# Attention and feed-forward on one core: 16-bit scores for two more batches, q and k loaded for two heads at a time

## The chip, the cores and the metric

The kernel runs on one core of a Trainium2 chip. The metric is the device time of one execution in microseconds (us). The core has five engines that work through rows of instructions of their own, in order: TensorE (PE, matrix products), VectorE (DVE), ScalarE (ACT), GpSimd (POOL) and SyncE (SP, which here issues the DMA transfers). They wait for one another by semaphores. SBUF is the on-chip memory of 128 partitions; PSUM holds the matrix products in banks.

## The reference

Attention in 8 batches of 8 heads, 576 positions, 64 values a head. A position sees all keys of its own block of 64 and of the blocks ahead of it. The heads' outputs of a position are put side by side (512 values), and a feed-forward layer follows.

```
scores = scale * q @ k^T                 # scale = 1/8
scores = where(block_i >= block_j, scores, -1e9)
attn   = exp(scores - max);  attn = attn / (sum(attn) + 1e-9)
x      = (attn @ v), heads side by side  # 4608 x 512
h      = x @ w_in                        # 512 x 2048
out    = max(0.01*h, h) @ w_out          # 2048 x 512
```

All inputs are 32-bit. q and k are large enough (about 0.57 in spread) that the products are made in several passes or parts.

## The kernel before

**Order.** The kernel is not written in the order in which it runs. `Plan` (lines 97 to 282) is a list scheduler: each piece of work is added with the engines that may do it, a cost in ns on each, a rank and the data it reads and writes. A replay of the costs then chooses engines and the row of instructions of every engine. The ranks are head positions plus constants (`RL` for loads of q and k, `RP` for their preparation, `RB` for late scores, and so on); the costs have constants too (`TURN`, `LOADC`, `TE`). Where the replay finds TensorE idle early in the program it puts in fills: matmuls of `ident` with itself whose result nobody reads (L1337).

**Work.** Batch 0 is done in two sets, "lo" (query rows 0 to 320 of each of the 8 heads) and "hi" (rows 320 to 576), batch 1 as "first" (rows 0 to 192) and "rest" (rows 192 to 576), batches 2 to 7 as "full" heads. The feed-forward layer of finished positions (L1129 and L1165) stands between the heads' work on TensorE. A head's q and k lie with the 64 values of a position on partitions; `z` is the parity of the head and chooses its buffer. Rest and full heads score their last 64 rows in a late block of its own.

**Scores, three ways.** Batch 0 and the first rows of batch 1 are in plain 32 bits, which is four passes a matmul (L696, L702). The host has put q and k on partitions 0 to 63 and again on 64 to 127, and for batch 0 the matmuls of one head go by turns to the two row halves of the array. Rest heads and batch 2 are below `SB` = 3: `before` holds q (`qs`) and k (`kk`) rounded to a 32-bit format with a single pass, high and low part above one another on 128 partitions (copies L328, subtractions L335), and the matmuls run over all 128 rows (L716, L721). Batches 3 to 7 are in 16 bits: two scaled copies and two low parts come from q and k, which the host has stored in both orders, and two DMAs swap the halves of the low part (L644, L645), so that three products of high and low parts run in two row halves at once (L710). Scales for them come from sums of squares of a head: a load of q and k of its own (L1047 squares them), totals over the partitions by two matmuls with `same` and `other` (L1054), once for four heads.

**Masks.** Where the scores are not in 16 bits, a matmul of `upper` with `far` adds a large negative number to the hidden corner (L691). For 16-bit heads VectorE writes the corner with a memset (L738). VectorE then takes row maxima (L747), ScalarE the exponentials (L764), and VectorE splits the normalised result into two 16-bit parts (L811).

**Weights.** Pieces of the two weight matrices come through `raw` and are reduced by ScalarE (L527, L528) and others early in the program; TensorE forms squares of them (L544).

Of the kernel before, what the change touches and what calls it, by code (L numbers as in the profile page):

```python
# [9 lines left out]
F32 = mybir.dt.float32  # L10
F32R = mybir.dt.float32r
# [8 lines left out]
P = 128  # L20
# [10 lines left out]
SIGNS = 3  # L31

# [6 lines left out]
TR = 0.745  # L39
TS = 1.212  # L40
TE = 59.721
# [3 lines left out]
AHEADQ = 5  # L45
RW = -1.068

RL = 4.584
RP = -0.167
RB = 0.488  # L50
RT = 1.469
RV = 2.065
RX = -8.245
RN = -2.665

LEAD = 4.25
LAG = 1.993
RS = 3.005
RG = 0.265
OFF1 = 4.712  # L60
OFF2 = -0.681
SL1 = 12.571
AHEAD = 0.967

LAT = 1550
HOLDP = 456.375
HOLD = 197.235
# [10 lines left out]
TURN = 90  # L78
# [7 lines left out]
SIDE = 34  # L86
STEPA = 0.46
STEPB = 0.457
VD = 3.329
JOINT = 0  # L90
DRATE = 330
SB = 3
RQ = 2.173
RD = 1.608
# [211 lines left out]
def attention_ffn(ctx: ExitStack, tc: tile.TileContext, qk0: bass.AP, qk: bass.AP, v: bass.AP, w_in: bass.AP, w_out: bass.AP, out: bass.AP):  # L306
# [11 lines left out]
    NQ = (B - SB) * H  # L318
# [31 lines left out]
    eighth = fixed([P, 2], F32, "eighth")  # L350
    nc.gpsimd.memset(eighth, 1.0)
    nc.gpsimd.memset(eighth[0:64, 0:1], scale)
    nc.gpsimd.memset(eighth[64:128, 1:2], scale)
# [27 lines left out]
    early = ctx.enter_context(tc.tile_pool(name="early", bufs=1))  # L381
    before = early.tile([P, 6 * S], F32R, name="before", tag="early")
    qs = [before[:, y * S : (y + 1) * S] for y in range(2)]
    kk = [before[:, 2 * (y + 1) * S : 2 * (y + 2) * S].rearrange("p (a b) -> p a b", a=2) for y in range(2)]
# [4 lines left out]
    for y in range(2):  # L389
        nc.gpsimd.memset(kk[y][64:128, 1].bitcast(F32), 0.0)  # L390
        nc.gpsimd.memset(sums[y], 1.0)
        nc.gpsimd.memset(nm[y], 0.0)
# [3 lines left out]
    v_raw = [fixed([P, GROUP, NT * D], F32, "v_raw"), raw.rearrange("p a b -> p (a b)")[:, : GROUP * NT * D].bitcast(F32).rearrange("p (h n) -> p h n", h=GROUP)]  # L396
    junk = fixed([P, GROUP * NT * D], BF16, "junk")
# [23 lines left out]
    for name, n in (("same", P // 2), ("other", P // 2), ("sn", NQ), ("qe", 2 * NQ), ("qsc", 2 * NQ), ("qin", 2 * NQ), ("qx", NQ)):  # L421
        later[name] = ptf[:, at : at + n].bitcast(BF16) if n == P // 2 else ptf[:, at : at + n]
        at += n
    q_raw = [raw.rearrange("p a b -> p (a b)")[:, GROUP * NT * D + S * y : GROUP * NT * D + S * (y + 1)].bitcast(F32) for y in range(3)]
# [41 lines left out]
    after, places, place_keys = [], {}, {}  # L466

    def again(k):
        if not after:
            after.append(early.tile([P, 6 * S], I32, name="after", tag="early"))  # L470
        return after[0][:, k * 2 * CH : (k + 1) * 2 * CH].bitcast(F16)

    found = [(lambda k=k: again(k), [(a, y) for a in ("qs", "kh", "kl") for y in range(2)]) for k in range(6)]
# [106 lines left out]
    def attention(i):  # L580
# [7 lines left out]
        qkt, qkey = qk_in[z], ("qkt", z)  # L588
        plain_s, plain_v = kind in ("lo", "hi", "first"), kind in ("lo", "hi")
        rows = P  # L590
        odd = kind == "lo" and z == 1
        sixteen = kind == "full" and b >= SB
        halves = sixteen or plain_v
        whole = scale if halves else scale / 2
# [17 lines left out]
        qf = qkt.rearrange("p a b -> p (a b)")  # L612
        at = qa if kind == "rest" else 0
        q_in, k_in = qf[:, at : at + nq], qf[:, at + nq : at + nq + ke]

        def load():
            if kind == "first":
                nc.sync.dma_start(qf[:, : 2 * nq].rearrange("p (a b) -> p a b", a=2), qk[b - 1, h][:, :, :nq])
            elif b:
                nc.sync.dma_start(qkt, qk[b - 1, h])  # L620
            else:
# [229 lines left out]
        if not JOINT and kind != "lo":  # L851
            normalise()
# [523 lines left out]
```

## Time and profile before

| | us |
|---|---|
| median of 3 runs | 1017.95 (1016.16 to 1018.43) |
| the profiled execution, its own time | 1018.16 |
| its span | 1016.0 |
| TensorE (PE) busy | 1003.3 (99% of the span) |
| VectorE (DVE) busy | 777.4 (77%) |
| ScalarE (ACT) busy | 729.9 (72%) |
| GpSimd (POOL) busy | 206.9 (20%) |

The span is the time from the first to the last event of the profile; 2.2 us lie around it. Matmuls are pipelined and their ends are modelled, so rows of the time line overlap a little: the time of a block of matmuls is read from its first start to the start of what follows it.

### The profile page before, as it was taken

To read this page: it belongs to the slowest core of one execution; us is meant where nothing else is said; L and a number is where in the kernel's file an instruction comes from. 1 tells how busy PE (TensorE), PEld (TensorE's weight loads), DVE (VectorE), ACT (ScalarE), POOL (GpSimd) and SP (SyncE) were. 2 spreads that over 40 slices of the span, in tenths; PEclk is the share of its full clock that TensorE was granted. 3 is DMA by queue.
4 is the path that set the end of the run, shared out by engine and by line. 5 is a ranking of instruction groups with operands and counts; after the bars stand their busy time and mean duration, and the time that the engine had idled before them with its cause. 6 is when DMAs were issued, how large, how long until landed. Compare 5 with 4: busy or idle time off the path is not lost.

```text
span 1016.0 us, 22617 instructions
## 1 busy us (share of the span) xinstructions
PE 1003.3 (99%) x8538; PEld 711.8 (70%) x8538; DVE 777.4 (77%) x2000; ACT 729.9 (72%) x1718; POOL 206.9 (20%) x279
## 2 busy tenths in 40 slices
PE   8999999999999999999999999999999999999997
PEld 7787766777666666666666666666666666788886
DVE  4688888899998888889988877866667578855454
ACT  4789877788878898888778878776567476533332
POOL 1001221123113334455422201131011021100010
PEclk9999999999999999999999999999999999999999
DMA  7766645988987898787779976883834535100000
GB/s 248 262 224 219 201 125 142 200 194 186 236 190 172 187 216 150 182 206 189 166 165 234 203 163 141 199 168 69 173 80 109 118 66 108 37 12 2 22 21 22
DMA packets 263181, 152.60 MB, mean 150 GB/s; under 512 B 223648, under 2 KB 240032, under 8 KB 263072
## 3 DMA queue, kind: packets, MB, share of 16 engines
q1 hardware_dynamic: 263072, 151.16, 62.9%
q8 instruction: 67, 1.10, 0.5%
q14 instruction: 42, 0.34, 0.1%
HBM read 80.74 MB, written 9.44 MB: 89 GB/s over the span
## 4 chain that ended last, share of the span: by engine, by line
PE 69%; ACT 2%; DVE 0%; issue 0%; DVEq 0%; ACTq 0%
PE p_h L1129 30%; PE p_o L1165 23%; PE p_s L710 5%; PE p_t L941 3%; PE p_o L1257 3%; PE p_s L1257 2%; PE p_t L963 2%; ACT slab L764 0%; ACT junk L1047 0%; ACT prow L764 0%; ACT slab L328 0%; PE p_s L721 0%; DVE slab L1270 0%; DVE ob L1270 0%; ACT junk L1019 0%
## 5 line engine op out<-in xcount | busy, mean ns | idle before, releaser
L1165 PE MATMUL p_o<-woh,ring 128*128 128x512 f16 x960 | 281.1, 379 | 0.0
L1129 PEld LDWEIGHTS <-wih 128*128 128x128 f16 x2432 | 226.3, 98 | 68.1 <-issue 17.1
L1165 PEld LDWEIGHTS <-ring 128*128 128x128 f16 (+1 forms) x1440 | 134.9, 98 | 135.4 <-issue 11.8
L1129 PE MATMUL p_h<-slab,wih 128*128 128x256 f16 (+1 forms) x1152 | 185.8, 267 | 0.0
L1129 PE MATMUL p_h<-xh,wih 128*128 128x256 f16 (+1 forms) x640 | 168.4, 268 | 1.4 <-ACT g L1134 1.3
L1134 ACT ACTIVATE g<-p_h 128x512 f32<-128x512 f32 (+1 forms) x152 | 86.8, 572 | 115.0 <-PE p_h L1129 112.1
L1129 PE MATMUL p_h<-xh,wil 128*128 128x256 f16 (+1 forms) x640 | 168.1, 267 | 0.0
L1129 PE MATMUL p_h<-xl,wih 128*128 128x256 f16 (+1 forms) x640 | 168.1, 267 | 0.0
L1129 PE MATMUL p_h<-slab,wil 128*128 128x256 f16 (+1 forms) x576 | 150.7, 267 | 0.0
L747 DVE TENSOR_REDUCE nm<-p_s 128x1 f32<-128x192 f32 (+4 forms) x308 | 137.4, 484 | 14.3 <-PE p_s L691 12.0
L1165 PE MATMUL p_o<-wol,ring 128*128 128x512 f16 x480 | 142.7, 379 | 0.0
L1129 PEld LDWEIGHTS <-wil 128*128 128x128 f16 x1216 | 118.9, 98 | 12.3
L336 POOL TENSOR_TENSOR ring<-g,ring 128x512 bf16<-128x512 f32 (+1 forms) x46 | 55.1, 1197 | 177.6 <-ACT ring L325 97.7
L811 DVE SCALAR_TENSOR_TENSOR slab<-prow,rec,slab 64x64 f16<-64x64 f32 (+4 forms) x148 | 80.7, 565 | 5.8 <-ACT slab L807 5.4
L335 DVE TENSOR_TENSOR ring<-g,ring 128x512 bf16<-128x512 f32 (+1 forms) x82 | 54.8, 668 | 33.0 <-ACT ring L325 32.4
L811 DVE SCALAR_TENSOR_TENSOR slab<-slab,rec 128x448 f16<-128x448 f32 (+4 forms) x132 | 73.3, 578 | 3.5 <-ACT slab L807 3.1
L764 ACT ACTIVATE slab<-p_s,nm,ptf 128x448 f32<-128x448 f32 (+4 forms) x100 | 60.5, 610 | 3.2 <-DVE nm L756 2.0
L764 ACT ACTIVATE prow<-p_s,nm,ptf 128x448 f32<-128x448 f32 (+4 forms) x100 | 60.4, 609 | 3.1 <-DVE nm L756 2.1
L325 ACT CAST ring<-g 128x512 f16<-128x512 f32 (+1 forms) x101 | 59.6, 591 | 1.9
L941 PEld LDWEIGHTS <-vs 128*128 128x128 f16 x968 | 49.6, 98 | 9.2 <-issue 4.6
L710 PE MATMUL p_s<-slab 64*128 64x320 f16 (+2 forms) x720 | 54.8, 276 | 0.0
L941 PE MATMUL p_t<-slab,vs 128*128 128x128 f16 (+1 forms) x968 | 54.2, 209 | 0.1
(234 smaller groups left out, 1725.1 us busy)
## 6 DMA issues: line engine op xcount, KB each, us to landing
qk_in<-in_qk SPq DMA_DIRECT2D x56, 576.0 KB, 4.6
raw<-in_qk SPq DMA_DIRECT2D x40, 288.0 KB, 3.5
raw<-in_w_in SPq DMA_DIRECT2D x16, 512.0 KB, 4.3
raw<-in_w_out SPq DMA_DIRECT2D x16, 512.0 KB, 4.4
slab<-slab SPq DMA_DIRECT2D x80, 72.0 KB, 4.3
out<-ob SPq DMA_DIRECT2D x19, 256.0 KB, 2.3
v_raw<-in_v SPq DMA_DIRECT2D x7, 640.0 KB, 4.5
raw<-in_v SPq DMA_DIRECT2D x7, 640.0 KB, 4.5
```

The lines of the kernel that those rows point to most:

```text
L325: one = lambda: nc.scalar.copy(dst(), src())
L335: ("DVE+" if sb else "DVE", dve(n) + 65, lambda: nc.vector.tensor_sub(dst(), one(), two())),
L336: ("POOL", pool2(n) - (0.25 * n if n == 512 else 0), lambda: nc.gpsimd.tensor_sub(dst(), one(), two())),
L710: go = lambda ap=ap, cols=cols, k0=k0, k1=k1, q_of=q_of, k_of=k_of, half_=half_, first=first, last=last: nc.tensor.matmul(ap, q_of[half_, ...
L747: [("DVE", dve(kw[t]), lambda t=t, ap=ap, flat=flat: nc.vector.tensor_reduce(nm[z][: qn[t], t : t + 1], ap[: qn[t]], axis=AX.X if flat els ...
L764: nc.scalar.activation(o, ap[: qn[t]], AF.Exp, bias=nm[z][: qn[t], t : t + 1], scale=whole if plain_s else esc[: qn[t]] if sixteen else 1. ...
L811: ("DVE+", dve(w) + 62, lambda: nc.vector.scalar_tensor_tensor(part(1), p, by, part(0), op0=ALU.mult, op1=ALU.subtract)),
L941: nc.tensor.matmul(p_t[x][:, c : c + src.free_size()], vs[z][:, (j + 1) % NT], src, start=start, stop=stop)
L1129: nc.tensor.matmul(hh[:, i, :n], w[:, f, d, :], x[:, d, :n], start=k == 0, stop=k == len(terms) - 1)
L1134: add([("ACT", act(2 * n), lambda: nc.scalar.activation(g[z][:, :, :n], hh[:, :, :n], AF.Prelu, alpha=0.01, scale=DOWN))], rank, [("h", z) ...
L1165: nc.tensor.matmul(p_o[m], a[:, i, m * P : (m + 1) * P], w[:, 2 * u + i, :], start=u == 0 and k == 0, stop=u == NU - 1 and k == 5,)
L1257: nc.tensor.matmul(acc(n), a[:, s, :], x()[w], start=u == 0 and k == 0, stop=u == NU - 1 and k == len(terms) - 1)
```

## The change

q and k come in a new layout from the host. For batch 0 and for the first 192 rows of batch 1 (`in_qk0`, `in_qk1`) each head lies on 64 partitions, and the kernel loads it to partitions 0 to 63 or 64 to 127 by its parity (`lanes`), into `spare`; the score matmuls use that half (`g = z`). For batches 1 to 7 q lies over k on 128 partitions, and one load brings two heads (`pair_in`, which takes the place of `q_group`) to one of three buffers. The same load serves the squares and the scores. The copies in the other order, the 32-bit tile `before` with its successor `after`, and the "side" layout of the scores are gone; a tile `spare` takes their place.

For every rest and full head one scaled copy `top` and one low part `low_` are made, and two DMAs of 64 partitions each swap the halves of both parts at once (576 positions of two 16-bit parts, 144 KB a transfer where 72 KB was before). Batches 1 and 2 score in 16 bits as the others do, with memsets as masks. Totals are formed for two heads at a time. New values of the rank and cost constants set another order of all instructions.

```
-TE = 59.721
+TE = 67.487
-RL = 4.584
+RL = 5.274
-HOLD = 197.235
+HOLD = 33.841
-TURN = 90
+BACK = 60
+TURN = 110
-SB = 3
...
-    early = ctx.enter_context(tc.tile_pool(name="early", bufs=1))
-    before = early.tile([P, 6 * S], F32R, name="before", tag="early")
+    spare = fixed([P, 6 * 2 * CH], I32, "spare")
+    qk_0 = [spare[:, 832 * y : 832 * (y + 1)].bitcast(F32) for y in range(2)]
...
-        sixteen = kind == "full" and b >= SB
-        halves = sixteen or plain_v
+        sixteen = not plain_s
...
+        qf, lanes = qk_0[z], slice(64 * z, 64 * z + 64)
...
+            nc.sync.dma_start(qf[lanes, : nq + ke], qk1[h] if kind == "first" else qk0[h, :, o : o + nq + ke])
...
-            add(copying(S, lambda: sx2, lambda: qkt[:, 1], by=cross), rp, [qkey, ("qsc", eq)], [k2])
-            add(copying(S, lambda: sx1, lambda: qkt[:, 0], by=mine), rp, [qkey, ("qsc", eq)], [k1])
...
-            add([("SP", 475, lambda: nc.sync.dma_start(sx3[0:64], sx4[64:128]))], rp, [k4], [k3], lag=dma(S * 64 * 2))
-            add([("SP", 475, lambda: nc.sync.dma_start(sx3[64:128], sx4[0:64]))], rp, [k4], [k5], lag=dma(S * 64 * 2))
...
-            add(copying(qe - qa, lambda: qd, lambda: q_in, by=eighth[:, 0:1]), rp, [qkey], [("qs", z)])
-            add(copying(ke, lambda: khd, lambda: k_in, by=eighth[:, 1:2]), rp, [qkey], [("kh", z)])
-            add(subtracting(qe - qa, lambda: qd[64:128], lambda: q_in[64:128], lambda: qd[64:128]), rp, [qkey], [("qs", z)])
-            add(subtracting(ke, lambda: kld[0:64], lambda: k_in[0:64], lambda: khd[0:64]), rp, [qkey, ("kh", z)], [("kl", z)])
+            add(copying(S, lambda: top, lambda: mine, by=by), rp, [qkey, ("qsc", eq)], [k1])
+            add([("DVE+", dve(S) + 62, lambda by=by: nc.vector.scalar_tensor_tensor(
+                low_, mine, by, top, op0=ALU.mult, op1=ALU.subtract
+            ))], rp, [qkey, ("qsc", eq), k1], [k2])
+            for y in range(2):
+                at, to = 64 * y, 64 - 64 * y
+                add([("SP", 475, lambda at=at, to=to: nc.sync.dma_start(qk16[z][to : to + 64, 2:4], qk16[z][at : at + 64, 0:2]))], rp, [k1, k2], [moved[y]], lag=dma(S * 64 * 4))
+            upside, low_side = (top, turned_[0]), (low_, turned_[1])
...
+                g = b if sixteen else z
...
-        for k in range(GROUP):
-            y = (GROUP * e + k) % 3
...
+        add([("SP", 475, lambda: nc.sync.dma_start(buf, qk[b - 1, h // 2]))], rank, [], [key] + first, lag=1.2 * dma(2 * S * P * 4))
+        add([("ACT", act(2 * S, True) + 94, lambda: nc.scalar.activation(
+            junk[:, : 2 * S], buf.rearrange("p a b -> p (a b)"), AF.Square, accum_out=sn[:, one]
+        ))], rank + RD, [key, "blocks"], [("sn", e), "junk"])
```

In the order of the program TensorE's fills go from 61 to 51 matmuls, the pairs of totals from 10 to 28, the squares of q and k from 40 operations on 576 columns to 28 on 1152, the loads for them from 40 to none beside the 28 of two heads, and the swaps from 80 to 112. In the new file the same statements have lower line numbers: L664 are all score matmuls and mask matmuls, L703 the exponentials (L764 before), L686 the maxima (L747), L750 the splitting (L811), L1047 the feed-forward's first product (L1129), L509 and L510 the weight pieces on ScalarE (L527, L528), L614 the low part, L679 the mask memsets, L1255 the fills (L1337).

The first excerpt is TensorE's row at the first scores of a rest head of batch 1; `slab_80` is the tile of the 16-bit parts. Before:

```order
L1129 MATMUL p_h_144<-slab_85,wil 128x256
L721 MATMUL p_s<-before 128x448 x2
L721 MATMUL p_s<-before 128x320 x2
L691 LDWEIGHTS upper
L691 MATMUL p_s<-far__78,upper 128x64
L691 LDWEIGHTS upper
L691 MATMUL p_s<-far__78,upper 128x64
L1129 LDWEIGHTS wih
```

After, at the same place:

```order
L1047 MATMUL p_h_135<-slab_81,wil 128x256
L664 LDWEIGHTS slab_80
L664 MATMUL p_s<-slab_80 128x320
L664 LDWEIGHTS slab_80
L664 MATMUL p_s<-slab_80 128x448
L664 LDWEIGHTS slab_80
L664 MATMUL p_s<-slab_80 128x320
L664 LDWEIGHTS slab_80
L664 MATMUL p_s<-slab_80 128x448
L664 LDWEIGHTS slab_80
L664 MATMUL p_s<-slab_80 128x320
L664 LDWEIGHTS slab_80
```

Four 128-row matmuls and two mask matmuls have become six matmuls in alternating row halves (the sixth stands behind the excerpt), with nothing else between.

The second excerpt is VectorE's row between two heads of batch 1; `p_s` is the score bank, `qk_in` the loaded q and k. Before:

```order
L335 TENSOR_TENSOR ring<-g_148,ring 128x512
L747 TENSOR_REDUCE nm_107<-p_s 128x1
L811 SCALAR_TENSOR_TENSOR slab_84<-prow_89,rec_111,slab_84 128x448
L335 TENSOR_TENSOR before<-qk_in_99,before 64x576 x2
L783 RECIPROCAL rec_111<-rec_111 128x1
```

After (the reduction of `nm_101` is the late one of a head, and the low part behind it belongs to the head after the next, which has the same buffer):

```order
L679 MEMSET p_s 64x64
L330 TENSOR_TENSOR ring<-g_139,ring 128x512
L686 TENSOR_REDUCE nm_101<-p_s 128x1
L614 SCALAR_TENSOR_TENSOR slab_81<-qk_in_95,ptf,slab_81 128x576
L750 SCALAR_TENSOR_TENSOR slab_81<-slab_81,rec_105 128x448
L750 SCALAR_TENSOR_TENSOR slab_81<-slab_81,rec_105 128x320
L722 RECIPROCAL rec_105<-rec_105 128x1
L679 MEMSET p_s 64x2x64
```

The low part has taken the place of the two subtractions, and memsets of the masks stand ahead of the reductions.

The third excerpt is the start of ScalarE's row; `prow` holds the first head's exponentials, `slab` and `raw` there are the first weight pieces. Before:

```order
L764 ACT_TABLE_LOAD
L764 ACTIVATE prow_88,sums_109<-p_s,nm_107 128x320
L764 ACTIVATE prow_87,sums_109<-p_s,nm_107 128x192
L764 ACTIVATE prow_86,sums_109<-p_s,nm_107 64x64
L527 ACTIVATE slab_84<-raw 128x512
```

After:

```order
L509 ACT_TABLE_LOAD
L509 ACTIVATE slab_80<-raw 128x512
L510 ACTIVATE raw<-raw 128x512
L703 ACTIVATE prow_84,sums_102<-p_s,nm_100 128x320
L703 ACTIVATE prow_83,sums_102<-p_s,nm_100 128x192
```

The first weight piece and the table load have moved ahead of the first exponentials.

## Rows read from the trace of the kernel before

**Rows 1.** Busy time by windows: us, PE, PEld, DVE, ACT, POOL, clock, DMA, GB/s.

```profile
20.00:140.00 120.00, 118.69 (x962) 93.13 (x962) 97.33 (x252) 100.56 (x248) 15.19 (x16) 1.00 0.64 204
140.00:300.00 160.00, 157.48 (x1286) 112.36 (x1284) 145.90 (x346) 129.12 (x309) 32.46 (x36) 1.00 0.86 191
```

**Rows 2.** Waits of TensorE, the longest entry: us in total, times, longest.

```profile
PE p_s L721 <- ACT slab L764: 2.2, 2, 1.3
```

**Rows 3.** TensorE's time line at a rest head: start, us, operation, count.

```profile
178.82 0.93 PE L721 MATMUL p_s<-before 128*128 128x448 f32 x4
179.60 0.23 PE L691 MATMUL p_s<-far__78,upper 128*128 128x64 bf16 x2
179.67 0.59 PE L1165 MATMUL p_o<-woh,ring 128*128 128x512 f16 x2
...
183.43 0.78 PE L721 MATMUL p_s<-before 128*128 128x288 f32 x4
...
184.09 0.59 PE L1165 MATMUL p_o<-woh,ring 128*128 128x512 f16 x2
```

**Rows 4.** The same at heads of batch 2, late block first.

```profile
247.08 0.38 PE L721 MATMUL p_s<-before 128*128 128x288 f32 x1
...
247.84 0.38 PE L1165 MATMUL p_o<-woh,ring 128*128 128x512 f16 x1
...
251.55 1.27 PE L721 MATMUL p_s<-before 128*128 128x448 f32 x6
...
252.77 0.27 PE L1129 MATMUL p_h<-xh,wih 128*128 128x256 f16 x1
```

**Rows 5.** The same at 16-bit heads of batch 3, late block first.

```profile
316.04 0.54 PE L710 MATMUL p_s<-slab 64*128 64x288 f16 x6
316.51 0.39 PE L1165 MATMUL p_o<-woh,ring 128*128 128x512 f16 x1
...
333.89 0.83 PE L710 MATMUL p_s<-slab 64*128 64x320 f16 x12
334.65 0.18 PE L1021 MATMUL p_t<-vn,ones 128*128 128x1 bf16 x1
```

**Rows 6.** The same in batch 0, a lo and a hi head.

```profile
28.80 0.80 PE L696 MATMUL p_s<-qk_in 64*128 64x320 f32 x6
...
29.57 0.33 PE L872 MATMUL p_t<-ident,prow 128*128 128x128 f32 x1
...
58.01 1.13 PE L696 MATMUL p_s<-qk_in 64*128 64x224 f32 x8
...
59.13 0.43 PE L918 MATMUL p_t<-ptf,vf 128*64 128x256 f32 x1
```

**Rows 7.** The same, attention times v of a hi head.

```profile
91.85 1.90 PE L918 MATMUL p_t<-ptf,vf 128*64 128x256 f32 x10
```

**Rows 8.** The same, a stretch of fills, and a pair of totals.

```profile
23.88 1.50 PE L1337 MATMUL p_o<-ident 128*128 128x128 f32 x12
...
309.38 0.20 PE L1054 MATMUL p_t<-ptf 128*128 128x4 bf16 x2
309.44 0.38 PE L1165 MATMUL p_o<-woh,ring 128*128 128x512 f16 x1
```

**Rows 9.** ScalarE's time line, its first instruction.

```profile
6.71 1.28 ACT L764 ACT_TABLE_LOAD   x1 [6.71 <-PE p_h L691]
```

**Rows 10.** Instructions of lines 721 and 641: ns min/median/max, first and last start.

```profile
L721 PE MATMUL p_s<-before x148: 191/309/554, 147.8 to 304.5; 128*128 128x288 f32 x64, 128*128 128x448 f32 x32, 128*128 128x320 f32 x32, 128*128 128x192 f32 x16
...
L641 DVE SCALAR_TENSOR_TENSOR slab<-qk_in,ptf,slab x40: 757/816/1381, 292.8 to 836.9; 128x576 f16<-128x576 f32 x40
```

**Rows 11.** DMA issues (KB, median us to landing), and line 645's landings.

```profile
qk_in<-in_qk SPq DMA_DIRECT2D x56, 576.0 KB, 4.6
...
slab<-slab SPq DMA_DIRECT2D x80, 72.0 KB, 4.3
...
DMA to landing us min/median/max: 2.0/4.2/7.0
```

More of the change, by code (lines that the diff above doesn't have):

```diff
@@ L724, in scores @@
-                yield RATE * (k1 - k0), go, LOADS
-        def softmax(tiles, mms, masks, r, sides=None):
+                    q_of, k_of = upper[half_], far[half_]
+                elif plain_s:
+                    q_of, k_of = q_in[half_, cols], k_in[half_, k0:k1]
+                else:
+                    cols = slice(q0[t], q0[t] + P)
+                    q_of, k_of = (low_side if c == 1 else upside)[b][half_, cols], (low_side if c == 2 else upside)[1 - b][half_, k0:k1]
+                go = lambda ap=ap, q_of=q_of, k_of=k_of, first=first, last=last: nc.tensor.matmul(ap, q_of, k_of, start=first, stop=last)
@@ L727, in softmax @@
+                yield price, go, TURN if y == 0 else LOADS if plain_s and t is not None else LOADC
+        def softmax(tiles, mms, masks, r):
             banks = sorted({(sk, bk) for _, _, bk in tiles for bk in bk})
@@ L828, in attention @@
         alias = ([6, 7] if z else [5, 4]) if kind == "first" else range(NT)
-        side = kind == "full" and i >= SIDE and not sixteen
-        order = "side" if side else f"first{z}" if kind == "first" else kind
+        order = f"first{z}" if kind == "first" else kind
         lay = order_a.get(order, ())
@@ L1025, in v_group, with pair_in @@
         add([("DVE+", 68, second)], rank, [("ve", e)], [("vin", e)])
-    def q_group(e):
-        i0 = next(i for i, (n, kind) in enumerate(work) if n == SB * H + GROUP * e and kind == "full")
+    def pair_in(e):
+        i0 = next(i for i, (n, kind) in enumerate(work) if n == H + 2 * e and kind in ("rest", "full"))
         b, h = divmod(work[i0][0], H)
         rank = pos[i0] - RL - RQ
-        same, other, sn, qe, qsc, qin, qx = later.values()
+        same, other, sn, qe, qsc, qx = later.values()
         if e == 0:
@@ L1051, in q_group @@
         x = bank()
         def total(y):
-            nc.tensor.matmul(p_t[x][:, GROUP * y : GROUP * y + GROUP], (same, other)[y], tops(sn[:, cols]), start=True, stop=True)
-        add([("PE", [(30, lambda y=y: total(y), LOADH) for y in range(2)])], rank + RD, [("sn", e, k) for k in range(GROUP)] + ["blocks"], [("t", x)])
-        add([("DVE", 75, lambda: halved(qe[:, two].bitcast(I32), p_t[x][:, : 2 * GROUP]))], rank + RD, [("t", x)], [("qe", e)])
-        first, second = powers(lambda: qe[:, two].bitcast(I32), lambda: qsc[:, two], lambda: qin[:, two])
@@ L1059, in q_group @@
-        add([("DVE+", 75, first)], rank + RD, [("qe", e)], [("qsc", e)])
-        add([("DVE+", 75, second)], rank + RD, [("qe", e)], [("qin", e)])
-        a, z = slice(two.start, two.start + GROUP), slice(two.start + GROUP, two.stop)
+            nc.tensor.matmul(p_t[x][:, y : y + 1], (same, other)[y], tops(sn[:, one]), start=True, stop=True)
+        add([("PE", [(30, lambda y=y: total(y), LOADH) for y in range(2)])], rank + RD, [("sn", e), "blocks"], [("t", x)])
+        add([("DVE", 75, lambda: halved(qe[:, two].bitcast(I32), p_t[x][:, :2]))], rank + RD, [("t", x)], [("qe", e)])
@@ L1358 @@
         "in_qk0": qk0,
+        "in_qk1": qk1,
         "in_qk": qk,
```

233 lines of the change are left out of this document (74 added, 159 removed).

## The prediction

> **What bounds the kernel now.** I read the busy time by stretches of the span first, then the list of TensorE's waits, then single score blocks on the time line of TensorE. TensorE is the bound nearly everywhere: it is busy 118.69 of the 120 us from 20 to 140 us and 157.48 of the 160 us from 140 to 300 us [rows 1]. VectorE, with 145.90 of 160 us, is the only other engine that comes close, and only in that second stretch. The longest entry in the list of TensorE's waits is 2.2 us, in two waits of the scores of batches 1 and 2 for an exponential that still holds the score bank [rows 2]. So a cost counts where it lands on TensorE's own row of instructions; work taken off ScalarE, VectorE or the DMA queues is worth only such waits as these. Everything below is therefore a sum over TensorE's row: the time from the first matmul of a block to the first one behind it, before and after.
>
> **Part a: scores of batch 1 (the eight "rest" heads) and batch 2 go to 16 bits.** Before, they are single-pass matmuls of rounded 32-bit data on all 128 rows. The block of a rest head takes 0.85 us (178.82 to 179.67) and its late block, the last 64 rows, 0.66 us (183.43 to 184.09) [rows 3]. A head of batch 2 takes 1.22 us (251.55 to 252.77) and 0.76 us (247.08 to 247.84) [rows 4]. Eight of each: 8 x (0.85 + 0.66) + 8 x (1.22 + 0.76) = 27.9 us. After, all sixteen run as the heads of batches 3 to 7 run already, three products, each in alternating 64-row halves: 0.76 us for the block of four row tiles (333.89 to 334.65) and 0.47 us for the late one (316.04 to 316.51) [rows 5]. Those blocks have 1536 and 864 columns per half, so a column costs (0.76 - 0.47) / 672 = 0.43 ns, and a rest head, with 1344 columns per half, comes to about 0.68 us. No mask matmuls remain; VectorE writes the masks. After: 8 x (0.76 + 0.47) + 8 x (0.68 + 0.47) = 19.0 us. **Part a: -8.9 us.** These heads' rows are known on both sides, so I put no more than 1 us of doubt on it.
>
> **Part b: batch 0 loses the second row half.** This part is easy to miss, since the diff speaks of a load. Batch 0 scores in plain 32 bits, four passes a matmul. Before, q and k lie on both halves of the partitions, and the score banks of one head are worked on in both row halves by turns: 0.77 us for 576 columns (28.80 to 29.57) and 1.12 us for 1024 columns (58.01 to 59.13) [rows 6]. After, a head's q and k lie on one half only (the half is the parity of the head), and all its score matmuls follow one another there. The trace has no 32-bit score block in one half. Its nearest row is another 32-bit four-pass block in one stretch of the array, the attention-times-v matmuls of batch 0: 1024 columns in a row that is 1.90 us long [rows 7]. Such a row is 0.07 us longer than the time to the next block's start, as rows 5 show (0.83 against 0.76), so 1.83 us, 1.79 ns a column. With 0.07 us for the two mask matmuls (179.60 to 179.67, rows 3), a "lo" head comes to 576 x 1.79 ns + 0.07 = 1.10 us and a "hi" head to 1.90 us. Bounds: below, no change, if the halves were no help before; above, twice the old block, if they were a full help, 8 x (0.77 + 1.12) = +15.1 us. I take the nearest row: 8 x (1.10 + 1.90) - 15.1 = **+8.9 us**, which is what part a brings.
>
> **Part c: totals.** A head's largest possible value is bounded from sums of squares. Two small matmuls form the totals: 0.06 us (309.38 to 309.44) [rows 8]. They come once for two heads now (28 times) and came once for four (10 times): 18 x 0.06 = **+1.1 us**.
>
> **Part d: fills.** The plan puts matmuls with no use into TensorE's row where it believes the engine idle. There are 61 of them in the order before and 51 after, and one in the order is two in the trace. Twelve take 1.50 us (23.88) [rows 8], so twenty are worth 2.5 us if useful work takes their place and nothing if a wait does. From 20 to 140 us TensorE lost only 1.3 us of 120 [rows 1], so what stood there was mostly due already; I take **-2.0 us**, between 0 and -2.5.
>
> **Part e: the start.** ScalarE loads its table for 1.28 us at 6.71 us, right when the first scores are done, and TensorE's transposes wait for the exponential behind it [rows 9]. In the new order the table load belongs to the first weight piece, ahead of the first scores. That can hide all of it (-1.3), or, if that piece lands late, put it and the piece's two operations (about the length of that load once more) ahead of the first exponential (+2). The loads for the first head are half as large. I take **-1.0 us**.
>
> **Part f: waits in batches 1 and 2.** The two waits of 2.2 us [rows 2] are of scores for a bank. The new scores stand in the same place, with fewer copies on ScalarE ahead of the exponentials; I take half, **-1.1 us**, between 0 and -2.2. What is next late there is VectorE, which loses two subtractions a head and gains one operation of 0.82 us [rows 10] and short mask writes. Fewer and larger loads, and 28 squares instead of 40 on ScalarE, I cost at nothing: they lie behind TensorE's row, which has work of the feed-forward layer while they run; if that cover went, each would cost a wait of its own length, 4.6 us for a load [rows 11].
>
> **The sum.** -8.9 + 8.9 + 1.1 - 2.0 - 1.0 - 1.1 = -3.0 us against the profiled execution's 1018.16 us: 1015.2 us. That execution is 0.2 us above the median of the runs shown, so the forecast is 1015.0 us. About 0.2%, 2 us, is what a measurement of this kernel can tell from no change: faster is below 1015.9, slower above 1020.0.
>
> **Rival 1, slower: the swaps are late.** In batches 1 and 2 the scores could start right behind the last copy; now they wait for two DMAs that swap halves of both 16-bit parts, issued behind the low part. The scores of those sixteen heads run from 147.8 to 304.5 us [rows 10], 9.8 us a head. In the order after, the low part of a head stands right behind the late reduction of the head that used the same buffer, so there is about one such period for 0.82 us of VectorE and the swap's flight: 9.0 us are left for the flight. Swaps of half the size land after 4.3 us in the middle and 7.0 us at most [rows 11]: a new one waits only if its flight grows with its size. Then the middle one takes 8.6 us and the longest 14.0, and the wait decides from 9.0 us on. With half of the sixteen heads late by 1 us in the mean that is +8 us, 1023.0 us. Against it: a load of eight times the bytes lands in 4.6 us [rows 11], so a flight does not go by bytes alone. For it: the DMA share is highest in this stretch, 0.86 [rows 1]. Behind TensorE's waiting score matmuls stand the feed-forward matmuls, so the wait costs its full length.
>
> The Trainium skill, "DMA: Bandwidth & Descriptors", section "Rules for kernel authors", speaks against two transfers to disjoint partition halves: it says that they share the same engines and so serialize, and advises one 128-partition transfer. By it the second swap would land a transfer behind the first. The trace shows nothing of it at half the size: the second swap lands after 4.2 us in the middle, both kinds together after 4.3 [rows 11].
>
> **Rival 2, more gain: neighbouring heads overlap.** Neighbours of batch 0 now lie in opposite row halves, so where two heads' score blocks stand next to each other the array could run them at once, as it ran the two halves of one head before. In the order after, two pairs of lo heads stand so. A pair then takes 2 x 0.77 instead of 2 x 1.10 us [rows 6, 7]: 2 x 0.66 = 1.3 us less, 1013.7 us. Against it: the pair's second head comes as a block behind the whole first one, not by turns, and the starts in the trace keep the order of the program, so little of it is side by side. The Trainium skill, "TensorEngine Tiling (Array Packing)", section "Tiling Modes", says that different tiles can load weights and multiply in parallel; by that rule the pairs would overlap. The trace bears it out only within a head, 0.77 us for 576 columns [rows 6].
>
> **Rival 3, no gain: the start is later.** The first weight piece lands behind the first scores, and the table load with its two operations stands ahead of the first exponential: +2.0 in place of -1.0, 1018.0 us. TensorE has nothing else to do then but fills and weight squares.
>
> **Rival 4, slower: part b costs its upper bound.** If one row half takes twice the old block, +15.1 in place of +8.9 us: 1021.2 us. Against it: the 1.79 ns a column of rows 7.
>
> **How the numbers follow.** The forecast has 0.50 (0.31 of it faster, 0.18 within, 0.01 slower), rival 1 0.20 (slower), rival 2 0.10 (faster), rival 3 0.15 (0.13 within, 0.02 slower), rival 4 0.05 (slower). That is faster 0.41, same 0.31, slower 0.28. The likeliest case's own range is 1011 to 1019: the sum with fills and waits at their better ends and part b 2 us lower, or with fills, waits and start at their worse ends. The range of 8 in 10 takes rival 1 in and goes down to parts a, b, d and f at their better ends together with rival 2: 1009 to 1024.
>
> **What would show it.** Right: a block of batch 0 takes 1.10 and 1.90 us in TensorE's time line, one of batches 1 and 2 0.76 or 0.68 and 0.47; no TensorE wait on a swap; table load before 5 us. Wrong: waits of the score line on the swap's DMA or on the low part between 140 and 300 us (rival 1); new waits anywhere behind 300 us, which I have at nothing; a lo block far from 1.10 us, the least certain price of the sum.

## The result, and the profile after

| | us | |
|---|---|---|
| median before | 1018.19 | 1016.16 to 1019.51, 4 runs |
| median after | 1032.56 | 1030.73 to 1033.03, 4 runs |
| ratio | 1.0139 | 95% interval 1.0126 to 1.0151 |

The changed kernel is 14 us slower; 3 us less were forecast, and 1024 was the upper end of the range. The profiled execution took 1032.97 us, with a span of 1031.0. Its first page says that TensorE is still the bound; the last matmul ends at 1025.40 us, and at 1010.35 in the kernel before.

The busy time by windows of the changed kernel (us, PE, PEld, DVE, ACT, POOL, clock, DMA, GB/s), as in rows 1, with the stretch behind them:

```profile
20.00:140.00 120.00, 120.00 (x884) 93.85 (x883) 96.51 (x239) 95.44 (x234) 12.42 (x13) 1.00 0.58 173
140.00:300.00 160.00, 157.71 (x1324) 100.57 (x1323) 132.41 (x366) 127.08 (x292) 46.37 (x56) 1.00 0.72 148
300.00:860.00 560.00, 555.30 (x4770) 361.10 (x4768) 450.09 (x1191) 418.04 (x1006) 162.66 (x204) 1.00 0.67 136
```

TensorE gets through 884 matmuls from 20 to 140 us, 962 in the kernel before [rows 1], and is busy all the time. VectorE is relieved from 140 to 300 us (132.41 against 145.90), the DMA share falls from 0.86 to 0.72, and nothing of that shows in the time. From 300 to 860 us TensorE idles 4.7 us, and 0.12 us in the kernel before:

```profile
300.00:860.00 560.00, 559.88 (x4777) 364.16 (x4776) 440.06 (x1177) 432.31 (x1032) 144.83 (x186) 1.00 0.72 158
```

TensorE's waits after, in all more than 0.5 us (us in total, times, longest), as in rows 2:

```profile
PE p_h L1047 <- DVE slab L1030: 2.8, 3, 1.6
PE p_s L664 <- ACT slab L703: 2.0, 6, 0.7
PE p_t L800 <- ACT prow L703: 1.4, 1, 1.4
PE p_o L1255 <- POOL ident masks.py:199: 1.4, 1, 1.4
PE p_t L974 <- DVE slab L832: 1.0, 1, 1.0
...
PE p_s L664 <- ACT prow L703: 0.7, 3, 0.3
PE p_t L869 <- DMA slab<-slab: 0.6, 2, 0.4
```

The longest single wait stands in the feed-forward rows, for VectorE's split of x, and the granted clock falls right behind it. TensorE's time line at that place, and the clock by windows:

```profile
353.45 0.37 PE L1047 MATMUL p_h<-slab,wih 128*128 128x256 f16 x1 [1.58 <-DVE slab L1030]
```

```profile
353.50:356.90 3.40, 3.40 (x25) 2.68 (x25) 3.27 (x7) 2.28 (x7) 2.37 (x3) 0.50 0.41 104
```

For these 3.4 us TensorE is at the lower of its two levels (1.2 of 2.4 GHz), and its matmuls take 1.6 us more than the same kinds do elsewhere in the trace (an estimate from their median distances). In the profile of the kernel before, the clock stays at its upper level from 12.7 to 1012.8 us.

No score matmul (L664) waits for a swap. The DMA issues (KB, median us to landing), as in rows 11:

```profile
slab<-slab SPq DMA_DIRECT2D x112, 144.0 KB, 3.8
qk_in<-in_qk SPq DMA_DIRECT2D x19, 576.0 KB, 5.2
raw<-in_qk SPq DMA_DIRECT2D x9, 576.0 KB, 5.0
```

A swap of twice the size lands after 3.8 us, sooner than the old one's 4.3 [rows 11].

The time line of TensorE at a lo and a hi head of batch 0, as in rows 6:

```profile
39.10 1.30 PE L664 MATMUL p_s<-spare 64*128 64x320 f32 x6
...
40.38 0.32 PE L853 MATMUL p_t<-ident,rec 64*64 64x64 f32 x2
...
47.68 1.99 PE L664 MATMUL p_s<-spare 64*128 64x224 f32 x8
...
49.66 0.33 PE L800 MATMUL p_t<-ident,prow 128*128 128x128 f32 x1
```

The lo block takes 1.28 us (0.77 before) and the hi block 1.98 us (1.12 before). Two lo heads side by side, in opposite row halves, take 2.25 us; the other such pair stands at the very start and waits for its load:

```profile
23.57 1.19 PE L664 MATMUL p_s<-spare 64*128 64x320 f32 x5
...
25.82 0.38 PE L1255 MATMUL p_o<-ident 128*128 128x128 f32 x1
```

And how a block of scores is entered, a late block of the last rest head (a late block has the last 128 query rows of a head, 448 to 576, not 64) and a main block of batch 2 in the changed kernel:

```profile
235.94 0.27 PE L1047 MATMUL p_h<-xh,wil 128*128 128x256 f16 x1
236.14 0.54 PE L664 MATMUL p_s<-slab 64*128 64x288 f16 x6
236.62 0.39 PE L1083 MATMUL p_o<-woh,ring 128*128 128x512 f16 x1
...
240.42 0.27 PE L1047 MATMUL p_h<-xh,wil 128*128 128x256 f16 x1
240.62 0.83 PE L664 MATMUL p_s<-slab 64*128 64x320 f16 x12
241.38 0.29 PE L869 MATMUL p_t<-slab,vs 128*128 128x128 f16 x2
```

and in the kernel before, the matmul ahead of the block of rows 3:

```profile
178.79 0.27 PE L1129 MATMUL p_h<-slab,wil 128*128 128x256 f16 x1
```

The blocks themselves are as forecast, 0.48 and 0.76 us; the main block of a rest head takes 0.67 us (157.98 to 158.65). But the first half-row matmul starts 0.20 us behind the start of the last 256-column feed-forward matmul, where the next feed-forward matmul would start 0.11 us behind it. The old full-row block starts 0.03 us behind it (178.79 to 178.82). A time from a block's first start to the next block's start leaves this out on one side and counts a piece of the feed-forward matmul in on the other. The distance goes with the part of the array that comes next: in both traces every undisturbed matmul of 128 rows and 128 columns but the single-pass 32-bit ones starts 0.11 us behind a 256-column feed-forward matmul, whatever its line and type, and the ones on a part of the array start 0.20 us behind it, the score matmuls in half rows as well as the transposes in half columns (L925, then L853).

Added up over TensorE's whole row (from each matmul's start to the next one's, by kind; the sum is the 15.05 us by which the last matmul ends later):

| kind | before | after | |
|---|---|---|---|
| score and mask matmuls | 98.7 | 101.4 | +2.7 |
| of it batch 0 | 16.3 | 27.6 | +11.3 |
| of it rest heads and batch 2 | 28.4 | 19.5 | -8.8 |
| feed-forward matmuls (L1129, L1165; then L1047, L1083) | 697.4 | 708.8 | +11.4 |
| fills | 20.2 | 18.1 | -2.0 |
| last matmuls of attention times v (L963; then L891) | 27.5 | 29.5 | +2.0 |
| totals | 0.6 | 1.7 | +1.1 |
| the rest | 164.4 | 164.3 | -0.1 |

The feed-forward matmuls are the same 5088. Their +11.4 us are, by the distance of each start to the next: +6.2 us at the change to scores, waits there counted in (before, 74 entries into half rows, each 0.096 us more than a plain distance, +7.1 us, and 31 into full rows, most of them 0.08 or 0.19 us less but three with a wait, +0.2 us together; after, 104 into half rows, +13.5 us, and none into full rows), +4.6 us inside the feed-forward rows (3.6 us of waits and 1.0 us of the slower clock from 353.5 us), and 0.6 us at other changes. The +2.0 us behind attention times v are waits of what comes next, 1.5 us of them two waits of a pair of totals (L974), whose result needs a bank that VectorE has not yet emptied (L832).

### The profile page after: what moved, and what is told of

It reads as the page before. It is cut to its first block, busy times and chain, and to the rows that moved or that the text cites. A ratio compares the mean times of both kernels' runs of the same rounds, so it can differ in the third digit from the quotient of the medians.

```text
span 1031.0 us, 22658 instructions
## 1 busy us (share of the span) xinstructions
PE 1014.0 (98%) x8584; PEld 705.9 (68%) x8584; DVE 785.3 (76%) x2054; ACT 717.8 (70%) x1683; POOL 238.5 (23%) x308
## 5 line engine op out<-in xcount | busy, mean ns | idle before, releaser
L1083 PE MATMUL p_o<-woh,ring 128*128 128x512 f16 x960 | 279.4, 380 | 0.1
L1047 PEld LDWEIGHTS <-wih 128*128 128x128 f16 x2432 | 225.5, 98 | 66.1 <-issue 18.8
L1083 PEld LDWEIGHTS <-ring 128*128 128x128 f16 (+1 forms) x1440 | 133.4, 98 | 141.3 <-issue 15.2
L1047 PE MATMUL p_h<-slab,wih 128*128 128x256 f16 (+1 forms) x1152 | 187.1, 268 | 2.8 <-DVE slab L1030 2.8
L1047 PE MATMUL p_h<-xh,wih 128*128 128x256 f16 (+1 forms) x640 | 168.7, 268 | 0.0
L1047 PE MATMUL p_h<-xh,wil 128*128 128x256 f16 (+1 forms) x640 | 168.3, 267 | 0.0
L1047 PE MATMUL p_h<-xl,wih 128*128 128x256 f16 (+1 forms) x640 | 168.3, 267 | 0.0
L1047 PE MATMUL p_h<-slab,wil 128*128 128x256 f16 (+1 forms) x576 | 151.4, 268 | 0.0
L686 DVE TENSOR_REDUCE nm<-p_s 128x1 f32<-128x192 f32 (+4 forms) x308 | 137.0, 484 | 16.3 <-PE p_s L664 13.5
L1083 PE MATMUL p_o<-wol,ring 128*128 128x512 f16 x480 | 142.8, 379 | 0.0
L1047 PEld LDWEIGHTS <-wil 128*128 128x128 f16 x1216 | 119.0, 98 | 15.9 <-issue 3.3
L331 POOL TENSOR_TENSOR ring<-g,ring 128x512 bf16<-128x512 f32 (+1 forms) x55 | 69.0, 1254 | 112.9 <-ACT ring L320 67.5
L703 ACT ACTIVATE slab<-p_s,nm,ptf 128x448 f32<-128x448 f32 (+4 forms) x132 | 81.2, 620 | 18.5 <-DVE nm L695 17.2
L703 ACT ACTIVATE prow<-p_s,nm,ptf 128x448 f32<-128x448 f32 (+4 forms) x132 | 81.2, 619 | 12.4 <-DVE nm L695 9.9
L750 DVE SCALAR_TENSOR_TENSOR slab<-prow,rec,slab 128x192 f16<-128x192 f32 (+4 forms) x148 | 83.5, 588 | 4.6 <-ACT slab L746 4.3
L664 PE MATMUL p_s<-slab 64*128 64x320 f16 (+2 forms) x960 | 76.1, 279 | 2.9 <-ACT slab L703 2.0
L750 DVE SCALAR_TENSOR_TENSOR slab<-slab,rec 64x64 f16<-64x64 f32 (+4 forms) x132 | 74.4, 587 | 4.2 <-ACT slab L746 3.9
L664 PEld LDWEIGHTS <-slab 64*128 64x128 f16 x960 | 38.4, 94 | 43.3 <-issue 30.8
L320 ACT CAST ring<-g 128x512 f16<-128x512 f32 (+1 forms) x109 | 64.5, 592 | 2.3
L330 DVE TENSOR_TENSOR ring<-g,ring 128x512 bf16<-128x512 f32 (+1 forms) x73 | 47.0, 644 | 17.8 <-ACT ring L320 17.1
```

What stands on the lines that cost most here:

```text
L320: one = lambda: nc.scalar.copy(dst(), src())
L330: ("DVE+" if sb else "DVE", dve(n) + 65, lambda: nc.vector.tensor_sub(dst(), one(), two())),
L331: ("POOL", pool2(n) - (0.25 * n if n == 512 else 0), lambda: nc.gpsimd.tensor_sub(dst(), one(), two())),
L664: go = lambda ap=ap, q_of=q_of, k_of=k_of, first=first, last=last: nc.tensor.matmul(ap, q_of, k_of, start=first, stop=last)
L686: [("DVE", dve(kw[t]), lambda t=t, ap=ap, flat=flat: nc.vector.tensor_reduce(nm[z][: qn[t], t : t + 1], ap[: qn[t]], axis=AX.X if flat els ...
L703: nc.scalar.activation(o, ap[: qn[t]], AF.Exp, bias=nm[z][: qn[t], t : t + 1], scale=scale if plain_s else esc[: qn[t]] if sixteen else 1. ...
```

## The experiments

The theory after the result was A: the loss is the price of matmul blocks, batch 0's single row half (10 to 11 us) and the entries into half rows, which take back most of the gain of the 16-bit scores, with some waits on top. The rival B: the blocks matter little and the new order of instructions loses the time.

**Batch 2 in 16 bits, alone, in the kernel before.**

```
-SB = 3
+SB = 2
```

> The kernel before with one number changed, SB = 2: batch 2 (8 heads) scores in 16 bits in two row halves, with the old loads and swaps; the rest heads of batch 1 stay as they were. Theory A (getting into a block of half-row matmuls costs what getting into a full-row block does not): in the traces of before and after, the first half-row score matmul starts 205 ns behind the start of the last 256-column feed-forward matmul, 312 ns behind a 512-column one, while the single-pass full-row one of before starts 28 ns behind it, so that a block read from its first start flatters the half-row kind by about 0.23 us. Then 8 x ((1.16 + 0.77) - (0.76 + 0.47)) = 5.6 us less, but 16 x 0.23 = 3.7 us of it goes into the entries: about 2 us faster, 1016. Rival B (the blocks' own times are right and the loss of the changed kernel is elsewhere): 5.6 us faster, 1012.6.

Measured: 1017.62 against 1018.53 us, ratio 0.9997 (0.9981 to 1.0012), so no change. In TensorE's row the score blocks are 5.3 us shorter, as their own times say, the feed-forward matmuls 4.7 us longer, of which 2.2 stand at the entries, waits there counted in (74 to 87 into half rows, 31 to 13 into full rows), and 2.5 are waits elsewhere in these rows. The gain that I read from the rows of blocks is there and is given back at the change of mode and in waits. Theory A had 2 us of gain, which is outside the interval by a little; new waits at other places (1.5 us for a transfer of P, 0.8 us for totals of v) are of the size of the rest.

**What the change between half and full rows costs.** A matmul of zeros stands in the middle of each 16-bit score block, once over all rows, once over the block's own half.

```
...
                 yield price, go, ...
+                if sixteen and y == 2:
+                    yield RATEH * BLK, lambda ap=ap, rows=slice(0, P): nc.tensor.matmul(ap[:, 0:BLK], zero[rows], far[rows], start=False, stop=False), LOADC
```

> The changed kernel with one more matmul of zeros, 128 rows by 64 columns, behind the third matmul of every 16-bit score block (112 blocks); it adds nothing to the scores, but the array goes from half rows to full rows and back. Theory A (a change between half and full rows has a price of 0.1 to 0.2 us): 112 x 0.15 to 0.3 = 17 to 34 us more, 1050 to 1066. Rival B (no such price): 112 x 0.03 = 3 us, 1036.

> The control of the run with the full-row zeros: the same matmul at the same place, but on the 64 rows of the block's own half, so the array stays in half rows. Both theories: 112 x 0.03 = 3 us more, or less where it hides beside the other half: 1032 to 1037.

Measured: 1065.54 us with the full-row zeros (ratio 1.0464, 1.0441 to 1.0487) and 1035.82 with the half-row ones (1.0172, 1.0152 to 1.0193). Over the changed kernel that is 33 us, 0.29 us for each of 112, against 3.3 us, 0.03 us each. The time line of a block with full-row zeros:

```profile
248.21 0.39 PE L666 MATMUL p_s<-slab 64*128 64x320 f16 x3
248.53 0.20 PE L669 MATMUL p_s<-far__76,zero 128*128 128x64 bf16 x1
248.66 0.64 PE L666 MATMUL p_s<-slab 64*128 64x64 f16 x9
249.23 0.60 PE L1087 MATMUL p_o<-woh,ring 128*128 128x512 f16 x2
```

and with half-row zeros:

```profile
243.66 0.39 PE L666 MATMUL p_s<-slab 64*128 64x320 f16 x4
243.89 0.19 PE L669 MATMUL p_s<-far__76,zero 64*128 64x64 bf16 x1
243.90 0.62 PE L666 MATMUL p_s<-slab 64*128 64x448 f16 x8
244.45 0.60 PE L1087 MATMUL p_o<-woh,ring 128*128 128x512 f16 x2
```

The same block takes 1.02 against 0.79 us, so going to full rows and back costs 0.23 us more than the same 64 columns in the block's own half. Over the whole kernel the difference of the two runs is 29.7 us, 0.27 us a block; some 2 us of it is the granted clock, which stands at its lower level for 10.2 us with the full-row zeros and 6.8 us with the half-row ones. A full-row matmul of 64 columns is not what costs; going there and back is. The Trainium skill has a rule for this: "TensorEngine Tiling (Array Packing)", section "Tiling Modes", says that a change of tiling mode drains the engine. The trace agrees and gives the price here, 0.1 us to enter half rows and 0.23 us there and back.

**Batch 0's row halves.** First with a new plan for it (a head's matmuls by turns in both halves, and the plan counting so):

```
-                g = b if sixteen else z
+                g = b if sixteen or plain_v else z
...
```

> The changed kernel with batch 0 again on both row halves: its q and k are loaded to all 128 partitions, and a head's score matmuls go by turns to both halves. All else as changed. Theory A: the block of a lo head goes back from 1.29 to 0.77 us and of a hi head from 1.98 to 1.13, 8 x (0.52 + 0.85) = 11 us less: 1021.6. Rival B (the new order of instructions is what loses; a shorter block only lengthens waits behind it): less than half of that, above 1027.

Measured: 1041.74 us, ratio 1.0225 (1.0205 to 1.0245), 9 us more than the changed kernel. The blocks did get shorter (a lo head 0.76, a hi head 1.13 us), but the planned order had 164 fill matmuls in the trace in place of 102, and the waits grew:

```profile
PE p_h L1047 <- DVE slab L1030: 6.0, 2, 3.2
PE p_s L664 <- ACT slab L703: 5.8, 6, 3.6
PE p_t L974 <- ACT junk L968: 1.5, 1, 1.5
```

It also lost by the clock. By windows:

```profile
261.90:268.70 6.80, 5.41 (x42) 3.71 (x41) 5.25 (x13) 2.50 (x6) 0.00 (x0) 0.50 0.73 183
354.10:371.10 17.00, 9.61 (x65) 5.47 (x65) 13.00 (x43) 14.62 (x35) 9.40 (x14) 0.50 0.45 106
```

The first stretch begins inside a wait of 2.8 us, the second inside one of 3.6 us. The matmuls in them take 7.8 us more than the same kinds elsewhere in the trace (an estimate from their median distances), where the changed kernel loses 1.6 us so. That run says little on the halves: it changed the order too. So the order was held. In the kernel before, batch 0 in one half, with every engine's row unchanged:

```
-                    half_ = slice(64 * b, 64 * b + 64)
+                    half_ = slice(64 * b, 64 * b + 64) if sixteen else slice(64 * z, 64 * z + 64)
```

> The kernel before with one thing changed: batch 0's score matmuls of a head all use the row half of the head's parity, as in the changed kernel. Every engine's row of instructions is the same, word for word. Theory A (batch 0's single half costs its full length on the path): blocks go from 0.76 to 1.29 and from 1.13 to 1.98 us, 8 x (0.53 + 0.85) = 11 us more, 1029.5. Rival B (what comes behind is bound by ScalarE, VectorE or the weights at that stage, and the fills and waits there give most of it back): under 5 us more, below 1023.5.

and in the changed kernel both halves, with its own order (the plan still counts with one):

```
...
-                half_, price = slice(64 * g, 64 * g + 64), begun[y + 1] - begun[y]
+                half_, price = slice(64 * (b if plain_v else g), 64 * (b if plain_v else g) + 64), begun[y + 1] - begun[y]
...
```

> The changed kernel with batch 0 on both halves again, but this time in the changed kernel's own order: the plan still counts with one half, so that every engine's row is the same, and only the halves of the score matmuls and the partitions of batch 0's loads differ. The run with a new order for this was 9 us slower than the changed kernel, though its blocks of batch 0 were 10 us shorter: it had 62 more fill matmuls and 20 us more of waits and entries in the feed-forward rows. Theory A: with the order held, the 11 us come back, 1021.6. Rival B: the blocks get shorter and waits take it back, above 1027.

Measured: 1029.27 us for the first, ratio 1.0101 (1.0084 to 1.0118), that is 10.3 us more than before, as theory A has it; its lo block:

```profile
31.30 1.30 PE L696 MATMUL p_s<-qk_in 64*128 64x320 f32 x6
...
32.59 0.33 PE L872 MATMUL p_t<-ident,prow 128*128 128x128 f32 x1
```

1025.19 us for the second, ratio 1.0067 (1.0052 to 1.0082): about 7.3 us of the 11 come back, between the two theories, and 3.7 us do not, among them fills (+2.1 us of TensorE's row), the transposes of P (+1.2) and others, which now wait. The row half is the largest single cause. Between this run and the one with the new plan only the order differs, and with it the count of fills, the waits and the clock behind them, and the time by 16.5 us: the plan's order is a cause of the same size as any edit here. About 6 us of the 16.5 are the clock (7.8 us lost by the estimate above, 1.5 us in this run).

One more run bears on the order: the changed kernel with the 26 rank and cost constants of the kernel before. Expected were 1028 to 1040 us if the prices of the blocks lose the time, and below 1024 us if the new constants do. It took 1045.70 us, ratio 1.0271 (1.0250 to 1.0291), slower than either, with the same blocks of batch 0 (1.29 and 1.98 us), longer waits, and 17.1 us at the lower clock from 354.4 us. Its output is wrong in that order, and why stays open, so its time is only a hint, against the new constants as what loses.

**The start.** In the changed kernel ScalarE's row begins so:

```profile
0.72 1.28 ACT L509 ACT_TABLE_LOAD   x1 [0.72 <-PEq L1288]
8.64 0.66 ACT L509 ACTIVATE slab<-raw 128x512 f32<-128x512 f32 x1 [6.63 <-DMA raw<-in_w_in]
9.20 0.64 ACT L510 ACTIVATE raw<-raw 128x512 int32<-128x512 uint8 x1
9.74 0.51 ACT L703 ACTIVATE prow<-p_s,nm 128x320 f32<-128x320 f32 x1
```

The table load is out of the way at 0.72 us, but the weight piece lands at 8.64 us, and the first exponential starts at 9.74 us. So the two operations were moved behind it (the list of closures is changed after the plan has made it):

```
...
+        piece, last = fns(self.spans), max(order.index(f) for f in fns(self.firsts[:3]))
+        order[:] = [f for f in order[: last + 1] if f not in piece] + piece + order[last + 1 :]
```

> The changed kernel with the first weight piece's two ScalarE operations (and the VectorE operation behind them) moved behind the first head's three exponentials, and a one-column exponential at the very start so that the table load stays there. All other rows are the same. Theory: the first exponential starts when the first scores are done, about 7.7 instead of 9.74 us, and the first attention-times-v block follows 2 us earlier, 1030.6. Rival: the weights or the second head set the time there, no change (1032.6).

Measured: 1032.71 us, no change. The first exponential starts at 7.38 us, 2.4 us sooner, but the first attention-times-v block at 16.00 instead of 16.38 us, and a wait of 0.9 us for the weight piece is new. The theory fell: the weights set the time there, and perhaps the second head, as the rival has it. The other way round, the early table load alone in the kernel before (one line ahead of the plan):

```
+    nc.scalar.activation(rec[0][:, 0:1], sums[0][:, 0:1], AF.Exp)
```

> The kernel before with a one-column exponential at the very start of ScalarE's row, which takes the table load of 1.28 us out of the wait for the first exponential. All other rows are the same. Theory: TensorE waited 0.9 us there and had two fills of no use ahead of the wait, so about 1.0 to 1.3 us less: 1017.3 against 1018.5. Rival: the second head's exponentials or the weight pieces set the time, no change.

Measured: 1015.98 against 1018.81 us, ratio 0.9971 (0.9960 to 0.9982), faster. Its ScalarE row:

```profile
0.73 1.28 ACT L393 ACT_TABLE_LOAD   x1 [0.73 <-PEq L1370]
...
6.64 0.53 ACT L765 ACTIVATE prow<-p_s,nm 128x320 f32<-128x320 f32 x1 [2.28 <-PE p_h L692]
```

The first exponential starts 1.4 us sooner than the table load of rows 9 let it (8.01 us), and TensorE's last matmul ends 1.8 us sooner in the trace. That is more than the 1.0 to 1.3 us of the theory; fills are 1.6 us shorter on TensorE's row, and the rest stays open. The kernel before could have had this part of the change without the rest.

**The fills.** In the changed kernel the fills are left out, the order is held.

```
-            nc.tensor.matmul(p_o[1][:, 0:P], ident, ident, start=True, stop=True)
+            pass
```

> The changed kernel without its 51 fill matmuls; all other rows are the same. It tests the term for fills: in the trace of the changed kernel they take 18.1 us of TensorE's row. Theory (fills stand where TensorE would wait): no change within 2 us, 1030.6 to 1034.6, and the same time shows as waits. Rival (fills delay the work behind them): up to 10 us faster. If the granted clock falls in the first 100 us, it is slower instead.

Measured: 1033.40 us, ratio 1.0153 (1.0136 to 1.0171): no change. The 18.1 us of fills show again as longer distances of their neighbours (the transposes of P +4.4, the squares of weights +3.8, scores +3.3 and so on). The clock falls too; from 20 to 60 us, by windows:

```profile
20.00:60.00 40.00, 37.40 (x245) 28.28 (x245) 26.28 (x72) 26.59 (x79) 0.00 (x0) 0.91 0.63 188
```

The granted clock is 0.91 in the mean there and 1.00 with the fills: it stands at 0.5 for 6.8 us from 25.6 us on, after a start in which TensorE was busy 14.18 of 20 us instead of 16.35. The matmuls of that stretch take 2.4 us more (an estimate as above). On the other hand the clock does not fall at 353 us in this run, though the wait there is the same. The two changes of the clock nearly cancel, and leaving the fills out wins nothing here.

**VectorE's part in the new waits.** 54 of the 56 low parts of q and k are left out (so the scores use stale low parts); all else is in place.

```
-            add([("DVE+", dve(S) + 62, lambda by=by: nc.vector.scalar_tensor_tensor(
+            add([("DVE+", dve(S) + 62, lambda by=by: n < H + 2 and nc.vector.scalar_tensor_tensor(
```

> The changed kernel with VectorE's low part of q and k left out from the third head of batch 1 on (54 of 56 operations of about 0.8 us, so the low parts of the scores are stale); the swaps still run, all other rows are the same. It tests whether the new waits inside the feed-forward rows (4.6 us more than before, the longest on VectorE's split of x) come from VectorE's added work. Theory: 3 to 5 us faster, 1027.6 to 1029.6, with most of these waits gone. Rival (they come from where the order puts the split of x and ScalarE's exponentials): less than 1.5 us faster.

Measured: 1027.11 us, ratio 1.0090 (1.0073 to 1.0107), some 5 us less than the changed kernel. TensorE's idle time from 300 to 860 us goes from 4.7 to 2.2 us:

```profile
300.00:860.00 560.00, 557.78 (x4814) 362.56 (x4812) 421.07 (x1154) 419.88 (x1010) 162.34 (x206) 1.00 0.66 137
...
353.50:356.90 3.40, 3.40 (x46) 2.38 (x43) 2.69 (x6) 3.30 (x8) 2.04 (x4) 1.00 0.91 266
```

The size is that of the theory, the mechanism is not. The waits inside the feed-forward rows go only from 3.6 to 3.0 us, and the longest, for the split of x near 350 us, stands as before. What goes is other waits (the scores' for exponentials from 2.7 to 0.8 us, the totals' from 1.5 to 0.3) and the stretch of slower clock, worth 1.6 us. So part of the new waits hang on VectorE's row. That they come from added work is not shown: batches 3 to 7 had the same 40 low parts before, with hardly a wait. Where in the new order VectorE falls behind stays open.

**A version that beats both.** The kernel before with the early table load and with batch 2 in 16 bits:

> The kernel before with both small edits: the early table load and batch 2 in 16 bits. If the two add up: the early table load was 2.9 us faster, batch 2 in 16 bits 0.3 us: 3.2 us less than the kernel before. If the start of the second set of waits takes it back, as in the run of batch 2 alone, no better than the table load by itself.

Measured: 1014.16 against 1017.96 us, ratio 0.9963 (0.9951 to 0.9975), 3.8 us faster than before and 18 us faster than the changed kernel. With 0.9971 for the table load alone, what batch 2 in 16 bits adds is not outside the intervals.

## Why the prediction was wrong

- **Part a** failed, and most in kind. The times of the blocks were right (0.48, 0.76 and 0.67 us; -8.8 us in TensorE's row where -8.9 stood). The step that failed is the one that took "the time from the first matmul of a block to the first one behind it" as the cost of a block. It leaves out how long the array needs to enter it. For half rows that is 0.1 us, for the old full-row blocks it was below zero, and 6.2 us of the 9 go back there, waits counted in. Rows 3 and 5 were read without the matmul ahead of them; the 0.20 us were in the trace before. The rule of the Trainium skill on a change of mode ("TensorEngine Tiling (Array Packing)", "Tiling Modes"), which the prediction left out, speaks against this part.
- **Part b** had the right mechanism and too small a size: 1.28 and 1.98 us a block where 1.10 and 1.90 stood, +11.3 us in TensorE's row where +8.9 stood. From the two blocks a column costs (1.98 - 1.28) / 448 = 1.6 ns, near the 1.79 taken, but a block has a fixed part of about 0.4 us (1.28 us less 576 columns at 1.56 ns), where 0.07 us was taken. With the order held it is worth 10.3 us. It is the largest single loss and far from the end that I took as "no change".
- **Part c** was right for the matmuls, +1.1 us. It put the waits of the pairs of totals at nothing: two of them wait 1.5 us for VectorE.
- **Part d** was right as a count (-2.0 us of TensorE's row) and wrong as a gain: even without any fill the time stays.
- **Part e** failed. The table load did move to 0.72 us, and the piece did land late, as rival 3 has it; with the piece moved behind the exponentials and the early load kept, the time stays. In the kernel before, where the piece already stands behind them, the early load alone won 2.8 us, so the gain is real there and does not reach the end here.
- **Part f** failed. The scores wait for exponentials 2.7 us in nine waits after, 2.4 in three before; and 3.6 us of new waits stand inside the feed-forward rows, what is "next late there" being VectorE. 1.0 us of them lies between 140 and 300 us, 2.6 us behind 300 us, where I had put nothing; there the slower clock behind one of them costs 1.6 us more, a cost that no term of the sum has.
- **Rival 1** was wrong: the flight did not grow with the size here (3.8 us at 144 KB, 4.3 at 72), and no score waits for one. **Rival 2** happens in small: two lo heads side by side take 2.25 us where 2.57 would be two of them, and two heads of the first rows of batch 1 0.99 us where 1.43 would be two. **Rival 4** was the nearest in sign and place, but one of three losses.
- On TensorE's row the sum missed by 18 us (15.05 later where 3.0 sooner stood): entries 6.2, waits and slower clock inside the feed-forward rows 4.6, batch 0 2.4, the gains of parts e and f that did not come 2.1, waits behind the last matmuls of attention times v 2.0, and small ones.

## What to carry to other kernels

Cost a block of matmuls from the start of the matmul ahead of it, not from its own first start: where the block uses another part of the array than its neighbours, getting in and out can be as much as the block saves. Test an edit of a planned kernel with the order held; a new order for the same work moved this one by 16 us. Look at the granted clock by windows wherever TensorE has waited: in some runs here it fell behind the wait, and the wait then cost more than its own length. And fills show idle time that something else sets: removing them won nothing here, and a shorter block next to them may only make more of them.

## What the runs showed of the hardware

- Going from half rows to full rows and back costs 0.23 us in a block and 0.27 us over the whole kernel, 112 times, against the same matmul in the block's own half.
- Behind a 256-column full-array matmul the next full-array one starts after 0.11 us, and one in half rows or half columns after 0.20 us.
- Two 32-bit blocks of neighbouring heads in opposite row halves overlap by 0.3 us of 2.57, and by 0.45 us of 1.43 where the blocks are shorter.
- Swaps of 64 partitions with 2304 bytes each land after 3.8 us in the middle, sooner than swaps of half that size did in the kernel before (4.3 us); from 300 to 860 us, where both kernels swap, the DMA share is 0.67 in place of 0.72.
- The granted clock fell to 0.5 behind waits of TensorE, for 3.4 us behind one of 1.6 us in the changed kernel and for 17 us in two runs whose longest waits are 3.6 and 3.7 us. The same wait at the same place was not followed by a fall in two other runs, so what decides it is not shown.
